# Attention and a two-layer feed-forward on one core: rounded score products for two more pairs, longer score runs, a later decay scaling and another order table

## The chip, the cores and the metric

The kernel runs on one core of one Trainium2 chip. The metric is the device time of one execution in microseconds (us). The engines are TensorE (PE; its weight loads are shown apart, as PEld), VectorE (DVE), ScalarE (ACT), GpSimd (POOL) and SyncE (SP), which here issues most DMA transfers.

## The reference

Eight batches of eight heads, 576 positions, head size 64. The attention has a decay: the logarithm of a gate `f` is summed along the sequence, and the difference of the sums at query and key is added to the score. The output of the attention, 4608 rows of 512, goes through two matrices with a leaky activation between them.

```python
scores = scale * np.matmul(q, k.transpose(0, 1, 3, 2))
log_f = np.log(np.clip(f, 0.0001, 1.0))
cum = np.cumsum(log_f, axis=-1)
decay = cum[:, :, :, None] - cum[:, :, None, :]
scores = np.where(causal, -1e9, scores + decay)
attn = np.exp(scores - scores.max(-1)); attn = attn / (attn.sum(-1) + 1e-9)
x = np.matmul(attn, v)            # then to (4608, 512)
h = x @ w_in
g = np.maximum(h, 0.0) + alpha * np.minimum(h, 0.0)
out = g @ w_out
```

## The kernel before

The work comes in 32 pairs: two heads of one batch, four pairs a batch. Eight batches make eight blocks of 512 rows for the feed-forward (the first 512 positions of each), and the last 64 positions of all batches make a ninth. `attention(n)` issues pair n, `ffn1(b)` the first matrix for block b, `ffn2(u)` the second.

A pair's queries are four tiles of 128 and a tail: tile i has 128(i+1) keys on or under the diagonal, so its scores are 128(i+1) columns for each head. The two heads' scores use 64 rows of the array each; the tail holds the last 64 queries of both heads and uses all 128 rows. Each tile then goes to DVE (line 830, tail line 680), which adds the decay and the mask from `Z` and takes the row extreme in one instruction, and to ACT (line 637) for the exponential and its sum. Pairs 0 to 7 turn the result by PE transposes through PSUM (line 651, `L876` for the tail), with evacuations on ACT and, for the first four pairs, partly on DVE (line 646). Pairs 8 and later turn it by DVE transposes and DMA. The values follow (`big,vr` or `wr,vr` in the rows), the division (`quotients`, line 939), and a split of the result into a rounded part (ACT, line 941) and the rest (POOL, line 943), which are the operands `xx` of the feed-forward.

Scores are computed in one of two ways. A pair under `NN` multiplies `q` and `k` as they are loaded (`rqk`), in float32. Another pair first splits them: ACT copies `q` and `k` into rounded tensors `Qh`, `Kh` (line 590), POOL subtracts to get the rest, `Ql`, `Kl` (line 595), and the scores are the sum of the three products Qh Kh, Qh Kl and Ql Kh; tile 0 of such a pair is done in float32 from a small copy (`qk`, lines 586 and 587). `NN` is 8 here, so pairs 0 to 7 use float32.

A run of scores is one planned operation on PE. `stretch` makes it for pairs under 8: for the first four (`NE`) tiles 0 and 1, then tile 2, then tile 3; for pairs 4 to 7 tiles 0, 1 and 3, then tile 2. Each tile of a run has its own PSUM, and tiles 2 and 3 use a bank per head.

The weights `w_in` come as 64-bit words and are converted block by block (`split64`, lines 364 to 377: four instructions on DVE, two on ACT, two on POOL for each of 16 blocks).

The order of work is made by a planner when the program is built. Every operation has an engine, an estimated duration, dependencies, buffers and a key. The planner takes, over all engines, the operation that can start first, and among those of one engine that could start alike the one with the lowest key. Pair n has key 10n plus offsets; the table `SHIFT` adds a number for each kind of step and pair: L loads, D decay, Z masks, S split, A scores, T transposes, V values, Q quotients, X outputs, W conversion of a weight block (key 40 + 2f for block f). Up to 82 us of its own planned time, where the planner sees a gap over 0.5 us before a PE operation that takes a new bank, it writes matmuls of the identity into it (line 479). The engines then run their queues in that order and wait for each other by semaphores.

The decay starts the program: `f` is loaded, clipped, its logarithm taken on ACT, and DVE sums along the sequence (line 403). DVE multiplies the sums by -8 (line 408), SP stores them to DRAM as `c8` (line 410), and five more DMAs regroup them there as `c8p` for pairs 8 and 9 (line 411). Pairs 1 to 7 read `c8` back, broadcast over the partitions (lines 533, 575). Pair 0 does not: PE spreads its sums from `cu` (line 523), and DVE adds the mask (line 550, `m1`).

Of the kernel before, what the change touches and what calls it, by code (L numbers as in the profile page):

```python
# [222 lines left out]
def attention_moe(  # L223
# [1170 lines left out]
```

## Time and profile before

| | |
|---|---|
| time, median of 3 runs | 991.21 us (990.93 to 991.32) |
| the profiled execution | 990.63 us, its span 988.8 us |
| PE busy | 982.2 us (99%) |
| DVE, ACT, POOL busy | 830.7, 614.4, 375.5 us |
| TensorE's granted clock | 1.000 of full speed over the span |

A busy share says how long an engine had an instruction under way, not whether the result was of use: a matmul of the identity in a gap counts as busy. Ends of matmuls are modelled, so the length of a run of matmuls overlaps the start of the next; from one row's start to the next row's start is how long PE was taken by it. An arrow in brackets gives the idle time before an instruction and what ended it.

### The profile page before, as it was taken

To read this page: it belongs to the slowest core of one execution; us is meant where nothing else is said; L and a number is where in the kernel's file an instruction comes from. 1 tells how busy PE (TensorE), PEld (TensorE's weight loads), DVE (VectorE), ACT (ScalarE), POOL (GpSimd) and SP (SyncE) were. 2 spreads that over 40 slices of the span, in tenths; PEclk is the share of its full clock that TensorE was granted. 3 is DMA by queue.
4 is the path that set the end of the run, shared out by engine and by line. 5 is a ranking of instruction groups with operands and counts; after the bars stand their busy time and mean duration, and the time that the engine had idled before them with its cause. 6 is when DMAs were issued, how large, how long until landed. Compare 5 with 4: busy or idle time off the path is not lost.

```text
span 988.8 us, 20133 instructions
## 1 busy us (share of the span) xinstructions
PE 982.2 (99%) x6935; PEld 827.5 (84%) x6935; DVE 830.7 (84%) x1585; ACT 614.4 (62%) x1399; POOL 375.5 (38%) x652
## 2 busy tenths in 40 slices
PE   9999999999999999999999999999999999999998
PEld 5777788888888888888888888999888988898898
DVE  6899988878787778779637988789999999999995
ACT  7888887878677686767635655645444543544352
POOL 5465976888868797777350000000000000000000
PEclk9999999999999999999999999999999999999999
DMA  7977768888888798796757655553444344334521
GB/s 216 260 215 259 251 217 247 254 246 262 247 251 255 224 261 249 219 267 200 215 180 237 203 172 200 174 170 107 149 128 149 107 149 155 122 107 149 169 67 43
DMA packets 133876, 191.68 MB, mean 194 GB/s; under 512 B 22647, under 2 KB 84590, under 8 KB 133774
## 3 DMA queue, kind: packets, MB, share of 16 engines
q1 hardware_dynamic: 128878, 175.73, 57.2%
q0 software_dynamic: 4608, 14.46, 5.3%
q8 instruction: 55, 0.90, 0.4%
q14 instruction: 47, 0.39, 0.1%
q10 hardware_dynamic: 288, 0.20, 0.1%
HBM read 102.95 MB, written 48.67 MB: 153 GB/s over the span
## 4 chain that ended last, share of the span: by engine, by line
PE 96%; DVE 2%; issue 1%; DMA 0%; ACT 0%; DVEq 0%; ACTq 0%
PE bank L381 93%; PE bank L651 2%; PE bank L444 0%; DMA wr<-in_w_in_dram 0%; DVE xs L939 0%; DVE hs L371 0%; DVE big L830 0%; PE bank L729 0%; PE bank L479 0%; DVE hs L1316 0%; DVE big L646 0%; DVE hs L368 0%; DVE wr L371 0%; DVE hs L367 0%; DVE wr L368 0%
## 5 line engine op out<-in xcount | busy, mean ns | idle before, releaser
L381 PE MATMUL bank<-xx,wi 128*128 128x512 f32 x1728 | 407.2, 392 | 0.0
L381 PEld LDWEIGHTS bank<-xx,wi 128*128 128x128 f32 x1728 | 320.4, 188 | 69.6 <-issue 3.0
L637 ACT ACTIVATE big<-big,st 128x384 f32<-128x384 f32 (+4 forms) x272 | 157.7, 582 | 25.8 <-DVE st L830 24.2
L1029 DVE SCALAR_TENSOR_TENSOR hs<-bank,sa,hs 128x512 f32<-128x512 f32 x116 | 86.5, 745 | 54.0 <-ACT hs L1027 52.5
L1027 ACT ACTIVATE hs<-bank,ab 128x512 f32<-128x512 f32 x116 | 79.7, 687 | 70.6 <-PE bank L381 69.0
L830 DVE CUSTOM_DVE_ANT_0 big<-bank,Z 128x384 f32<-128x384 f32 (+1 forms) x220 | 93.0, 480 | 34.2 <-PE bank L381 27.7
L1268 ACT ACTIVATE xx<-gj 128x1792 fp32r<-128x1792 f32 x37 | 62.4, 1701 | 95.0 <-DVE gj L1261 57.3
L381 PE MATMUL bank<-wot,xx 128*128 128x256 f32 (+1 forms) x734 | 120.6, 323 | 0.0
L381 PE MATMUL bank<-wi,xx 128*128 128x256 f32 (+1 forms) x734 | 120.6, 323 | 0.0
L381 PEld LDWEIGHTS bank<-wi,xx 128*128 128x128 f32 x734 | 106.8, 189 | 12.2
L381 PEld LDWEIGHTS bank<-wot,xx 128*128 128x128 f32 x734 | 106.8, 189 | 12.2
L846 DVE STREAM_TRANSPOSE big<-big 128x768 f32<-128x768 f32 x96 | 90.3, 959 | 8.5 <-ACT big L637 8.5
L543 POOL TENSOR_TENSOR Z<-Z,tri 128x128 f32<-128x128 f32 x192 | 79.8, 444 | 34.3 <-DVE Z L513 30.7
L1269 DVE TENSOR_TENSOR xx<-gj,xx 128x1792 fp32r<-128x1792 f32 x37 | 74.4, 2018 | 2.5 <-ACT xx L1268 2.5
L943 POOL TENSOR_TENSOR xx<-xs,xx 128x256 fp32r<-128x256 f32 x64 | 49.0, 781 | 43.2 <-ACT xx L941 42.7
L381 PEld LDWEIGHTS bank<-big,vr 128*64 128x64 f32 x1168 | 53.7, 137 | 9.1 <-issue 5.5
L381 PE MATMUL bank<-wi,gh 128*128 128x256 f32 (+1 forms) x370 | 60.9, 322 | 0.0
L381 PE MATMUL bank<-wot,gh 128*128 128x256 f32 (+1 forms) x370 | 60.9, 322 | 0.0
L381 PE MATMUL bank<-big,vr 128*64 128x128 f32 (+1 forms) x1168 | 59.7, 260 | 0.0
L381 PEld LDWEIGHTS bank<-wot,gh 128*128 128x128 f32 x370 | 53.9, 189 | 6.0
L381 PEld LDWEIGHTS bank<-wi,gh 128*128 128x128 f32 x370 | 53.9, 189 | 6.0
L1298 ACT ACTIVATE hs<-bank 128x256 f32<-128x256 f32 x102 | 36.5, 384 | 24.9 <-PE bank L381 24.6
(164 smaller groups left out, 1585.6 us busy)
## 6 DMA issues: line engine op xcount, KB each, us to landing
hd<-hs SPq DMA_DIRECT2D x144, 256.0 KB
gj<-hd SPq DMA_DIRECT2D x50, 512.0 KB
rqk<-in_qk_dram SPq DMA_DIRECT2D x28, 512.0 KB
wx<-hd SPq DMA_DIRECT2D x22, 512.0 KB
vr<-in_vv_dram SPq DMA_DIRECT2D x32, 320.0 KB
wr<-in_w_in_dram SPq DMA_DIRECT2D x16, 512.0 KB
wx<-in_w_out_dram SPq DMA_DIRECT2D x16, 512.0 KB
out_dram<-hs SPq DMA_DIRECT2D x30, 256.0 KB
```

The costliest lines, as they stand in the source:

```text
L381: pe.matmul(o, lhsT, rhs, start=start, stop=stop)
L543: ms.append(op("POOL", c_po(128), lambda to=to, i=i, zd=zd: po.tensor_tensor(to()[:, :, -1:], zd()[:, :, i : i + 1], tk(), ALU.add), kc + ...
L637: ex = op("ACT", c_exp(w), lambda: ac.activation(at(bt.t), at(bt.t), AF.Exp, bias=lo()[:, col : col + 1], scale=-1.0, accum_out=su()[:, co ...
L651: pe.transpose(t[:, c : c + 128], src[:, 128 * j : 128 * j + 128], ident)
L830: ve.tensor_tensor_reduce(out=o if turned else blk(o), in0=blk(bS.t[:, c0 : c0 + w]), in1=in1(), scale=-0.125, scalar=3.0e38, op0=ALU.add, ...
L846: ve.transpose(part(b_[:, 0 : 768 if k < 3 else MW]), part(bE.t[:, c0 : c0 + (768 if k < 3 else MW)]))
L943: xl = op("POOL", c_po(256), lambda r=r, t0=t0: po.tensor_tensor(bx.t[:, 1, t0 : t0 + 256], bxs[r].t[:, 0:256], bx.t[:, 0, t0 : t0 + 256]. ...
L1027: cp = op("ACT", c_act(512), lambda bh=bh, bs=bs, fc=fc: ac.activation(bs.t, bh.t, AF.Relu, scale=ab[:, fc : fc + 1]), -1000, [last, o_sg] ...
L1029: cp = op("DVE", c_dve(512), lambda bh=bh, bs=bs, fc=fc: ve.scalar_tensor_tensor(bs.t, bh.t, sa[:, fc : fc + 1], bs.t, ALU.mult, ALU.add), ...
L1268: hi = op("ACT", c_acs(896 * GW), lambda w=w, bgh=bgh: ac.activation(bgh.t[:, 0], w(), AF.Copy), key, [o2], [bj, bgh])
L1269: lo = op("DVE", c_dve(896 * GW), lambda w=w, bgh=bgh: tt(bgh.t[:, 1], w(), bgh.t[:, 0].bitcast(F32), ALU.subtract), key + 0.1, [hi], [bj, ...
L1298: side = op("ACT", c_act(256), lambda m=m, slot=slot: ac.activation(bs.t[:, slot], bo[m].t[:, 256:512], AF.Copy), kd, [last], [bo[m], bs])
```

## The change

- `NN` goes from 8 to 6: pairs 6 and 7 split `q` and `k` and score by three rounded products, tile 0 in float32. Their split on POOL is cut in three pieces, and the small copy for tile 0 takes the first 128 keys, as these pairs' keys stand in plain order.
- Pairs 0 to 3 get the score runs that pairs 4 to 7 have.
- The multiplication by -8, the store of `c8` and the regrouping are issued after pair 0's operations, and the multiplication also waits for pair 0's first masked decay.
- The instruction that brings ACT's table for the exponential reads its own cell, not the decay's buffer.
- The table `SHIFT` has other numbers throughout.

```diff
-NN = 8
+NN = 6
...
-SHIFT = {
+SHIFT = {
...
-('A', 3): 165.1
-('A', 4): 13.0
-('A', 6): 173.3
-('A', 7): 218.4
+('A', 3): -13.3
+('A', 4): 74.5
+('A', 6): 1.9
+('A', 7): 70.1
...
-    o_warm = op("ACT", 1500, lambda: ac.activation(warm, ft()[0:1, 0:1], AF.Exp), -99, o_ln, [bft])
+    o_warm = op("ACT", 1500, lambda: ac.activation(warm, warm, AF.Exp), -99, o_ln)
...
-    o_8 = [op("DVE", 150 + (a1 - a0) / 1.92, lambda a0=a0, a1=a1: ve.tensor_scalar_mul(ft()[:, a0:a1], cu()[:, a0:a1], -8.0),
-              -100, [o_sc[i]], [bcu, bft]) for i, (a0, a1) in enumerate(PC)]
-    o_c8 = op("SP", 400, lambda: sy.dma_start(c8, ft()), -49, o_8, [bft], kb=147)
-    o_c8p = [...
...
+                first_m.append(m1)
...
-                    k0_().rearrange("p (k x) -> p k x", k=4), k_()[:, 0:512].rearrange("p (k x) -> p k x", k=4)[:, :, 0:32]), kc, l_qk, [bqk, bQ])]
+                    k0_().rearrange("p (k x) -> p k x", k=4), (k_()[:, 0:512].rearrange("p (k x) -> p k x", k=4)[:, :, 0:32] if n >= NX[0] else k_()[:, 0:128].rearrange("p (k x) -> p k x", k=4))), kc, l_qk, [bqk, bQ])]
...
-                short = turned and i == 0
+                short = len(terms) > 3 and i == 0
...
-        for tiles in ((0, 1), (2,), (3,)) if n < NE else ((2, 3, 0, 1),) if turned else ((0, 1, 3), (2,)):
+        for tiles in ((0, 1, 3), (2,)) if n < NE else ((2, 3, 0, 1),) if turned else ((0, 1, 3), (2,)):
...
     attention(0)
     op("-", 0, lambda: setattr(plan, "fill", fill), 0, [o_id] + first_up)
+    plan.at("", 0)
+    o_8 = [op("DVE", 150 + (a1 - a0) / 1.92, lambda a0=a0, a1=a1: ve.tensor_scalar_mul(ft()[:, a0:a1], cu()[:, a0:a1], -8.0),
+              -100, [o_sc[i], first_m[0]], [bcu, bft]) for i, (a0, a1) in enumerate(PC)]
+    o_c8 = op("SP", 400, lambda: sy.dma_start(c8, ft()), -49, o_8, [bft], kb=147)
+    o_c8p = [...
```

## Rows read from the trace of the kernel before

**Rows 1.** Page, part 1: busy us (share of the span) x instructions, by engine

```profile
PE 982.2 (99%) x6935; PEld 827.5 (84%) x6935; DVE 830.7 (84%) x1585; ACT 614.4 (62%) x1399; POOL 375.5 (38%) x652
```

**Rows 2.** Busy time by stretches: window, us, then each engine's busy us

```profile
40.00:59.00 19.00, 17.71 (x191) 13.42 (x189) 18.26 (x45) 13.69 (x39) 11.23 (x14) 1.00 0.70 223
59.00:97.00 38.00, 38.00 (x296) 29.63 (x296) 34.65 (x82) 34.28 (x95) 26.05 (x32) 1.00 0.77 243
97.00:124.00 27.00, 26.48 (x176) 20.56 (x176) 24.33 (x42) 22.69 (x59) 26.18 (x32) 1.00 0.81 256
145.00:545.00 400.00, 400.00 (x3224) 332.89 (x3223) 304.39 (x746) 280.20 (x789) 277.40 (x492) 1.00 0.81 238
```

**Rows 3.** Timeline of PE, pair 2's three runs: start us, length us, what

```profile
23.85 0.93 PE L381 MATMUL bank<-rqk 64*128 64x128 f32 x8
...
25.73 0.92 PE L381 MATMUL bank<-rqk 64*128 64x384 f32 x4
...
28.90 1.13 PE L381 MATMUL bank<-rqk 64*128 64x512 f32 x4
```

**Rows 4.** Timeline of PE, pair 6's scores and what follows them

```profile
77.04 1.78 PE L381 MATMUL bank<-rqk 64*128 64x128 f32 x12
78.75 0.28 PE L729 MATMUL bank<-ident,st 128*9 128x128 f32 x1
...
82.65 0.60 PE L381 MATMUL bank<-rqk 128*128 128x256 f32 x2
83.09 0.49 PE L651 MATMUL bank<-ident,big 128*128 128x128 f32 x3
83.42 0.70 PE L381 MATMUL bank<-rqk 128*128 128x320 f32 x2
83.96 0.27 PE L729 MATMUL bank<-ident,st 128*9 128x128 f32 x1
...
88.93 0.92 PE L381 MATMUL bank<-rqk 64*128 64x384 f32 x4
```

**Rows 5.** Timeline of PE, a later pair's rounded scores: first row, and next work

```profile
160.39 0.39 PE L381 MATMUL bank<-Kh,Qh 64*128 64x256 f32 x2
...
163.31 8.35 PE L381 MATMUL bank<-xx,wi 128*128 128x512 f32 x36
```

**Rows 6.** Timeline of PE, 45 to 60 us: stalls, identity matmuls, first feed-forward

```profile
45.53 0.83 PE L479 MATMUL bank<-ident 128*128 128x128 f32 x6
...
48.66 0.66 PE L651 MATMUL bank<-ident,big 128*128 128x128 f32 x4 [0.33 <-ACT big L637]
...
50.68 0.66 PE L651 MATMUL bank<-ident,big 128*128 128x128 f32 x4 [0.93 <-ACT big L637]
...
51.91 1.83 PE L479 MATMUL bank<-ident 128*128 128x128 f32 x14
...
59.01 1.66 PE L381 MATMUL bank<-xx,wi 128*128 128x512 f32 x6
```

**Rows 7.** One tile's instructions (rqk): count, ns minimum/median/maximum, first and last start

```profile
L590 ACT ACTIVATE Qh<-rqk x24: 615/619/628, 97.4 to 465.9; 128x512 fp32r<-128x512 f32 x24
...
L590 ACT ACTIVATE Kh<-rqk x24: 668/672/680, 97.9 to 467.2; 128x576 fp32r<-128x576 f32 x24
L595 POOL TENSOR_TENSOR Ql<-rqk,Qh x24: 1267/1298/1720, 98.1 to 471.3; 128x512 fp32r<-128x512 f32 x24
L595 POOL TENSOR_TENSOR Kl<-rqk,Kh x24: 1404/1435/1869, 99.7 to 472.5; 128x576 fp32r<-128x576 f32 x24
```

**Rows 8.** Timeline of all engines, opening: decay scaling and pair 1's first mask

```profile
6.13 0.62 DVE L408 TENSOR_SCALAR big<-big 64x256 f32<-64x256 f32 x2 [0.20 <-ACT warm L401]
...
6.77 0.43 DVE L550 TENSOR_TENSOR Z<-bank,tri 128x256 f32<-128x256 f32 x1
...
13.22 0.67 POOL L557 TENSOR_TENSOR Z<-Z,tri 128x256 f32<-128x256 f32 x1 [2.33 <-DMA Z<-c]
```

**Rows 9.** One line's instructions: DVE's L368, ns minimum/median/maximum

```profile
L368 DVE SCALAR_TENSOR_TENSOR hs<-wr,hs x8: 692/749/1105, 43.3 to 125.2; 128x512 uint32<-128x512 uint32 x8
```

More of the change, by code (lines that the diff above doesn't have):

```diff
@@ L54 @@
 KD, KE = 100.55, 102
-SHIFT = {('L', 0): 9.4, ('D', 0): 2.2, ('Z', 0): 60.6, ('A', 0): 2.2, ('T', 0): -0.3, ('V', 0): -13.3, ('Q', 0): 36.2, ('X', 0): -10.8, ('L', 1): 26.8, ('D', 1): 1.4, ('Z', 1): -27.5, ('A', 1): 47.1, ('T', 1): 17.0, ('V', 1): 48.8, ('X', 1): 122.0, ('L', 2): 28.7, ('D', 2): 45.5, ('Z', 2): 10.6, ('A', 2): 54.0, ('T', 2): 1.8, ('V', 2): 58.1, ('Q', 2): -44.8, ('X', 2): 24.9, ('L', 3): 15.8, ('D', 3): -69.7, ('Z', 3): 0.9, ('A', 3): 165.1, ('T', 3): -84.7, ('Q', 3): 0.7, ('D', 4): -10.7, ('Z', 4): 63.2, ('A', 4): 13.0, ('T', 4): 4.2, ('V', 3): 35.9, ('Q', 4): 132.1, ('X', 3): -15.3, ('L', 5): 81.7, ('D', 5): -4.2, ('Z', 5): -0.4, ('A', 5): 21.2, ('T', 5): -65.7, ('V', 4): 1.3, ('Q', 5): -3.4, ('X', 4): 18.4, ('L', 6): 69.8, ('D', 6): 30.4, ('A', 6): 173.3, ('T', 6): 64.2, ('V', 5): 16.9, ('L', 7): 15.0, ('D', 7): -6.8, ('Z', 7): -95.9, ('A', 7): 218.4, ('T', 7): 47.3, ('V', 6): -17.7, ('V', 7): -37.7, ('Q', 7): -7.0, ('X', 5): -14.8, ('X', 6): -7.2, ('W', 0): 14.3, ('W', 1): 178.8, ('W', 2): 130.1, ('W', 3): -7.0, ('W', 4): 29.0, ('W', 5): 13.1, ('W', 6): 131.9, ('W', 7): -0.1, ('W', 8): -24.7, ('W', 9): 48.7, ('W', 10): -21.0, ('W', 11): -226.7, ('W', 12): -27.8, ('W', 13): 9.3, ('W', 14): 110.8, ('W', 15): 19.8, ('L', 8): -132.0, ('D', 8): -70.2, ('Z', 8): -11.8, ('S', 8): 10.0, ('A', 8): 59.0, ('L', 9): 6.4, ('D', 9): -6.1, ('Z', 9): 32.3, ('S', 9): -81.3, ('A', 9): -1.9, ('Q', 9): -96.4, ('X', 7): 3.1, ('L', 10): 50.1, ('Z', 10): 7.2, ('S', 10): 75.8, ('A', 10): -14.4, ('V', 8): -29.5, ('L', 11): 6.9, ('Z', 11): 41.4, ('S', 11): -6.8, ('A', 11): -68.7, ('V', 9): 12.9, ('Q', 11): 10.9, ('X', 8): 37.3, ('X', 9): 119.6, ('L', 12): 6.3, ('Z', 12): -18.6, ('S', 12): 23.7, ('A', 12): -9.9, ('V', 10): -2.9, ('L', 13): 2.6, ('Z', 13): -3.7, ('S', 13): 27.4, ('A', 13): 27.1, ('V', 11): -0.8, ('Q', 13): -134.7, ('X', 10): 5.7, ('X', 11): 5.8, ('L', 14): 1.6, ('Z', 14): 459.3, ('S', 14): -32.6, ('A', 14): -10.4, ('V', 12): 1.0, ('L', 15): 34.3, ('Z', 15): 17.4, ('S', 15): 96.4, ('A', 15): -40.5, ('V', 13): -69.9, ('Q', 15): -38.3, ('X', 13): 4.3, ('L', 16): 2.7, ('Z', 16): -198.9, ('S', 16): -187.7, ('A', 16): 154.9, ('V', 14): -18.6, ('L', 17): -9.2, ('Z', 17): 0.6, ('S', 17): 49.4, ('A', 17): -109.5, ('Q', 17): -229.2, ('X', 14): 26.2, ('X', 15): -29.2, ('L', 18): -40.0, ('Z', 18): -30.3, ('S', 18): 19.5, ('A', 18): -44.4, ('V', 16): 8.7, ('L', 19): -4.1, ('Z', 19): 16.8, ('S', 19): -29.0, ('A', 19): -99.9, ('V', 17): -19.8, ('Q', 19): -113.9, ('X', 16): 4.8, ('X', 17): -2.5, ('L', 20): -18.2, ('Z', 20): -4.1, ('S', 20): 3.5, ('A', 20): -15.6, ('V', 18): -13.2, ('L', 21): 24.2, ('Z', 21): -5.1, ('S', 21): 30.9, ('A', 21): 1.5, ('V', 19): -12.3, ('Q', 21): -6.5, ('X', 18): -66.7, ('X', 19): 21.5, ('L', 22): -197.2, ('Z', 22): -25.6, ('S', 22): -118.4, ('A', 22): 52.2, ('V', 20): 46.3, ('L', 23): 3.6, ('Z', 23): 49.0, ('S', 23): 3.0, ('A', 23): -4.3, ('V', 21): 106.1, ('Q', 23): -43.7, ('X', 20): 27.7, ('X', 21): -18.4, ('L', 24): -6.9, ('Z', 24): 91.0, ('S', 24): 17.4, ('A', 24): 103.3, ('V', 22): -23.4, ('L', 25): -7.9, ('Z', 25): 14.7, ('S', 25): -51.9, ('A', 25): 20.7, ('V', 23): 21.8, ('Q', 25): 14.2, ('X', 22): 35.9, ('X', 23): -3.3, ('L', 26): -42.8, ('Z', 26): 29.2, ('S', 26): 11.4, ('A', 26): 78.5, ('V', 24): 156.6, ('L', 27): -38.3, ('Z', 27): 1.9, ('S', 27): 40.9, ('A', 27): 0.5, ('Q', 27): 2.0, ('X', 24): -6.8, ('X', 25): 12.5, ('L', 28): -1.5, ('Z', 28): -21.7, ('S', 28): 28.1, ('A', 28): -23.8, ('V', 26): 13.8, ('L', 29): 6.3, ('Z', 29): -5.4, ('S', 29): -109.1, ('A', 29): -4.1, ('V', 27): -32.8, ('Q', 29): -0.6, ('X', 26): -3.0, ('X', 27): -14.3, ('L', 30): -20.4, ('Z', 30): 3.6, ('S', 30): 13.5, ('A', 30): 40.4, ('V', 28): 9.6, ('L', 31): -7.6, ('Z', 31): -99.0, ('S', 31): 13.9, ('A', 31): -1.5, ('V', 29): 16.7, ('V', 31): 16.3, ('V', 30): -2.0, ('Q', 31): -48.0, ('X', 28): -51.3, ('X', 29): -14.3, ('X', 30): -12.2, ('X', 31): -79.3}
@@ new lines @@
+SHIFT = {('L', 0): 10.0, ('D', 0): 94.6, ('Z', 0): 8.1, ('A', 0): 78.0, ('T', 0): -16.6, ('V', 0): -26.9, ('Q', 0): -47.4, ('X', 0): 116.6, ('L', 1): 21.9, ('D', 1): 109.0, ('Z', 1): -11.9, ('A', 1): 7.3, ('T', 1): -9.1, ('V', 1): -9.5, ('Q', 1): 2.2, ('X', 1): 49.7, ('L', 2): -10.2, ('D', 2): 208.8, ('Z', 2): -23.4, ('A', 2): 5.6, ('T', 2): 268.3, ('V', 2): 33.8, ('Q', 2): -11.8, ('X', 2): -52.6, ('L', 3): 71.1, ('D', 3): 156.3, ('A', 3): -13.3, ('T', 3): 36.7, ('Q', 3): 19.2, ('L', 4): 0.1, ('D', 4): 35.5, ('Z', 4): 47.7, ('A', 4): 74.5, ('T', 4): -56.5, ('V', 3): 0.8, ('Q', 4): -23.7, ('X', 3): 138.0, ('L', 5): 24.5, ('D', 5): -35.8, ('Z', 5): -11.4, ('A', 5): 143.4, ('T', 5): -38.8, ('V', 4): 183.4, ('Q', 5): -48.8, ('X', 4): 55.9, ('L', 6): 162.4, ('D', 6): -18.8, ('Z', 6): 15.2, ('S', 6): -52.8, ('A', 6): 1.9, ('T', 6): -266.1, ('V', 5): -7.1, ('L', 7): -28.9, ('D', 7): 86.5, ('Z', 7): -11.4, ('S', 7): -16.2, ('A', 7): 70.1, ('T', 7): 121.7, ('V', 6): 496.0, ('V', 7): -3.1, ('Q', 7): -41.8, ('X', 5): 198.8, ('X', 6): 54.2, ('W', 0): -63.0, ('W', 1): 384.4, ('W', 2): 117.4, ('W', 3): -12.1, ('W', 4): 171.4, ('W', 5): 120.2, ('W', 6): -145.9, ('W', 7): -49.0, ('W', 8): 31.1, ('W', 9): -37.8, ('W', 10): -0.6, ('W', 11): 110.4, ('W', 12): 4.9, ('W', 13): -13.9, ('W', 14): -11.3, ('W', 15): 47.0, ('L', 8): 416.4, ('D', 8): -19.3, ('Z', 8): 4.1, ('S', 8): -34.1, ('A', 8): 198.7, ('L', 9): -41.2, ('D', 9): -46.3, ('Z', 9): -5.5, ('S', 9): 192.4, ('A', 9): -9.5, ('Q', 9): -33.8, ('X', 7): 39.0, ('L', 10): 6.5, ('Z', 10): 37.1, ('S', 10): 76.4, ('A', 10): -57.8, ('V', 8): 3.5, ('L', 11): 62.0, ('Z', 11): -43.5, ('S', 11): 77.1, ('A', 11): -0.2, ('Q', 11): -47.7, ('X', 8): 5.7, ('X', 9): -25.3, ('L', 12): -33.0, ('Z', 12): 13.1, ('A', 12): 31.0, ('V', 10): 29.9, ('L', 13): -4.4, ('Z', 13): -13.6, ('S', 13): -5.3, ('A', 13): -4.4, ('V', 11): 1.0, ('Q', 13): -10.5, ('X', 10): 17.6, ('L', 14): 50.0, ('Z', 14): 87.5, ('S', 14): 6.4, ('A', 14): -16.8, ('V', 12): -28.4, ('L', 15): -175.7, ('Z', 15): 105.2, ('S', 15): 12.3, ('A', 15): 4.9, ('V', 13): -44.6, ('Q', 15): 5.6, ('X', 12): -95.8, ('X', 13): 98.2, ('L', 16): 22.6, ('Z', 16): 0.8, ('S', 16): 24.1, ('A', 16): -141.7, ('V', 14): 29.7, ('L', 17): 24.8, ('Z', 17): -5.1, ('S', 17): -139.9, ('A', 17): 15.8, ('V', 15): 0.5, ('Q', 17): 18.8, ('X', 14): -20.0, ('X', 15): -29.9, ('L', 18): 41.8, ('Z', 18): -12.8, ('S', 18): 10.7, ('A', 18): -4.1, ('V', 16): 6.5, ('L', 19): -81.0, ('Z', 19): -6.3, ('S', 19): 17.9, ('A', 19): 21.7, ('V', 17): 0.1, ('Q', 19): -94.5, ('X', 16): 32.4, ('X', 17): 22.1, ('L', 20): -5.3, ('Z', 20): -10.0, ('S', 20): 3.0, ('A', 20): -10.3, ('V', 18): 25.8, ('L', 21): -43.3, ('Z', 21): 51.2, ('S', 21): 4.0, ('A', 21): 8.9, ('V', 19): -0.8, ('Q', 21): -14.1, ('X', 18): 17.7, ('X', 19): -12.0, ('L', 22): -37.2, ('S', 22): 2.5, ('A', 22): 6.3, ('V', 20): 15.6, ('L', 23): 88.2, ('Z', 23): -20.9, ('S', 23): 164.0, ('A', 23): 75.0, ('V', 21): -20.9, ('Q', 23): 13.1, ('X', 20): 86.4, ('X', 21): -23.2, ('L', 24): 0.8, ('Z', 24): 9.6, ('S', 24): 253.1, ('A', 24): -6.8, ('V', 22): 0.8, ('L', 25): 93.5, ('Z', 25): -3.8, ('S', 25): -1.2, ('A', 25): 22.1, ('V', 23): 21.4, ('Q', 25): -98.9, ('X', 22): -3.5, ('X', 23): 23.4, ('L', 26): -23.3, ('Z', 26): 21.9, ('S', 26): -1.4, ('A', 26): -1.0, ('V', 24): 58.8, ('L', 27): -7.2, ('Z', 27): -27.4, ('S', 27): 39.4, ('A', 27): -134.6, ('V', 25): -44.8, ('Q', 27): 0.7, ('X', 24): -12.7, ('X', 25): -35.8, ('L', 28): -0.2, ('Z', 28): -4.3, ('S', 28): 44.6, ('A', 28): 16.1, ('V', 26): -62.7, ('L', 29): 61.4, ('Z', 29): -2.9, ('S', 29): -2.9, ('A', 29): -27.8, ('V', 27): 4.8, ('Q', 29): -24.6, ('X', 26): -2.4, ('X', 27): 24.0, ('L', 30): 4.7, ('Z', 30): 29.4, ('S', 30): 9.7, ('A', 30): -1.9, ('V', 28): -191.9, ('L', 31): -14.6, ('Z', 31): -35.7, ('S', 31): 24.9, ('A', 31): -22.1, ('V', 29): -25.0, ('V', 31): 0.8, ('V', 30): 39.1, ('Q', 31): -16.4, ('X', 28): -6.5, ('X', 29): 6.8, ('X', 30): 24.7, ('X', 31): -32.2}
@@ L406, in attention_moe @@
     o_scan = o_sc[1]
-    o_8 = [op("DVE", 150 + (a1 - a0) / 1.92, lambda a0=a0, a1=a1: ve.tensor_scalar_mul(ft()[:, a0:a1], cu()[:, a0:a1], -8.0),
-              -100, [o_sc[i]], [bcu, bft]) for i, (a0, a1) in enumerate(PC)]
-    o_c8 = op("SP", 400, lambda: sy.dma_start(c8, ft()), -49, o_8, [bft], kb=147)
-    o_c8p = [op("SP", 400, lambda k=k: sy.dma_start(c8p[:, 128 * k : 128 * k + 128].rearrange("p (s c) -> p s c", c=32),
-                                                    c8[:, 0:512].rearrange("p (s k c) -> p s k c", k=4, c=32)[:, :, k]), 6, [o_c8], kb=60) for k in range(4)]
-    o_c8p.append(op("SP", 400, lambda: sy.dma_start(c8p[:, 512:S], c8[:, 512:S]), 6, [o_c8], kb=16))
     o_id = op("POOL", 600, lambda: make_identity(nc, ident), -98)
@@ L479, in fill @@
             pe.matmul(bank[:, 0:128], ident, ident, start=True, stop=True)
-    first_up = []
+    first_up, first_m = [], []
     x_ops, x_late, xt_ops, s_0 = {}, [], [], []
@@ L1036, in attention_moe @@
     op("-", 0, lambda: setattr(plan, "fill", fill), 0, [o_id] + first_up)
+    plan.at("", 0)
+    o_8 = [op("DVE", 150 + (a1 - a0) / 1.92, lambda a0=a0, a1=a1: ve.tensor_scalar_mul(ft()[:, a0:a1], cu()[:, a0:a1], -8.0),
+              -100, [o_sc[i], first_m[0]], [bcu, bft]) for i, (a0, a1) in enumerate(PC)]
+    o_c8 = op("SP", 400, lambda: sy.dma_start(c8, ft()), -49, o_8, [bft], kb=147)
+    o_c8p = [op("SP", 400, lambda k=k: sy.dma_start(c8p[:, 128 * k : 128 * k + 128].rearrange("p (s c) -> p s c", c=32),
+                                                    c8[:, 0:512].rearrange("p (s k c) -> p s k c", k=4, c=32)[:, :, k]), 6, [o_c8], kb=60) for k in range(4)]
+    o_c8p.append(op("SP", 400, lambda: sy.dma_start(c8p[:, 512:S], c8[:, 512:S]), 6, [o_c8], kb=16))
     o_sg = None
```

## The prediction

> **What bounds the kernel now.** I read the page's busy line first, then the busy time by stretches of the span, then TensorE's order of instructions in the opening. TensorE (PE) is busy for 982.2 of 988.8 us [rows 1]. By stretches it is full between 59 and 97 us and from 145 to 545 us, and it misses 1.29 us at 40 to 59 and 0.52 us at 97 to 124 [rows 2]. The reader is to see two regimes. From 59 us on, PE always finds something, because the feed-forward of batch 0 lies ready as a stock of work: there a microsecond taken off PE's own instructions is a microsecond off the end. Before 59 us the busy share deceives. The planner writes matmuls of the identity into gaps (line 479); they count as busy and compute nothing. Before pair 3's last transposes and behind them PE shows 0.83 and 1.83 us of such matmuls and 0.33 and 0.93 us of idleness that ends with an exponential on ACT [rows 6]: 3.9 us in which PE waits for pairs 3 and 4. In that stretch DVE is busy for 18.26 of 19.00 us [rows 2], so the waiting is for DVE and for what ACT makes of DVE's output.
>
> **The change part by part.** All terms are made against the profiled execution's own time, 990.63 us (its span of 988.8 and 1.83 around it), which is 0.58 under the median of 991.21; I add that 0.58 at the end.
>
> *Pairs 6 and 7 by rounded products.* Removed: the float32 scores. For pair 6 these are the run of tiles 0, 1 and 3 from 77.04 to 78.75 (1.71 us), the tail's two parts, 82.65 to 83.09 and 83.42 to 83.96 (0.44 and 0.54), and tile 2, 0.92 long, less the 0.07 by which the first run's length overlaps what follows (1.78 against 1.71), 0.85 [rows 4]: 3.54 us. Added: three rounded products per tile, tile 0 staying float32. A later pair that already does this, tails included, runs from 160.39 to 163.31 [rows 5]: 2.92 us. So 0.62 us a pair, 1.2 us in all, on PE, in the stretch in which it is full. Bounds: the whole lengths of the float32 rows (1.78, 0.60, 0.70, 0.92) sum to 4.00, which would give 1.08 a pair and 2.2 us; if the products of pairs 6 and 7 are broken up between other work and lose their overlap, nothing is left. I take -1.2, the start-to-start reading, since PE's next instruction begins there.
>
> *Their cover.* The split of q and k is new for these two pairs: on ACT two copies of 0.62 and 0.67 us, on POOL two subtractions of 1.30 and 1.44 us, here in three pieces each [rows 7], and a small copy on each engine. That is at least 2 x 1.29 = 2.6 us of ACT and 2 x 2.74 = 5.5 us of POOL; at the longest durations of those rows POOL takes 2 x 3.59 = 7.2 us. I cost them at nothing: PE has the feed-forward of batch 0 to do meanwhile, and the results are needed by PE only. If that cover is gone, up to 5.5 us (7.2 at most) comes back. It is thin on one side: POOL is busy for 26.18 of 27.00 us at 97 to 124, but for 26.05 of 38.00 at 59 to 97 [rows 2], so it matters whether the table puts the split early. It does: the keys of the scores are 10 per pair plus the table's entry, for pair 6 233 before and 62 after, for pair 7 288 and 140.
>
> *The first four pairs in two runs.* Pair 2's three runs last 0.93, 0.92 and 1.13 us [rows 3], 2.98 together; pair 6's two for the same tiles 1.78 and 0.92 [rows 4], 2.70. So 0.28 us a pair, 1.1 us for four. But PE waits in this stretch anyway, so a part only makes its wait longer; between 0 and -1.1 I take -0.5. Against it: a run of tiles 0, 1 and 3 asks for four banks of PSUM at one time, where each run asked for two.
>
> *The new table.* It decides the order of everything before 545 us. What I can tie to a row: pair 3 is the last that batch 0's feed-forward needs, and its scores had key 30 + 165 = 195, behind pair 4's 40 + 13 = 53; now they have 17 against 115. The stall of 3.9 us [rows 6] is the wait for pairs 3 and 4, and DVE there alternates between them and the weights' conversion. Bounds: all of the 3.9 recovered, or as much again lost where another pair comes late in its place. I take -1.0, a quarter of it, because DVE's own work, 18.26 of 19.00 us [rows 2], is not removed and only its order changes.
>
> *The decay scaling later.* The two multiplications by -8 (0.62 us on DVE [rows 8]) move behind pair 0's first masked decay, so the store of the scaled decay and pair 1's broadcasts of it, all on SP's queue, leave later, and so do the five regrouping copies behind them. POOL waited 2.33 us for the first of those broadcasts [rows 8], so pair 1's masks come later by nearly what the store does: 0.43 us for the masked decay that now goes ahead [rows 8], plus at most one 0.62. Pair 0 gains at most the 0.62. Bounds -0.6 to +1.1 us; I take +0.2, nearer to zero, because PE is still busy with pair 0 when pair 1's masks land. The activation-table warm-up reads its own cell instead of the decay; it stays behind the logarithms on ACT, and I cost it at nothing: it hides behind the scan on DVE, and without that cover it is inside the 0.6 already counted.
>
> Sum: 990.63 - 1.2 - 0.5 - 1.0 + 0.2 = 988.1 us, and with 0.58 for the median 988.7 us, a gain of 2.5 us or 0.25%. About 0.2%, 2.0 us, is what a measurement of this kernel can tell from no change, so faster means under 989.2 and slower over 993.2.
>
> **The rivals.** *Nothing is won before 59 us:* the order changes, the wait moves to another pair, and only the rounded products remain: 991.2 - 1.2 = 990.0 us. For it speaks that DVE is nearly full at 40 to 59; against it, that 2.66 us of PE's time there is identity matmuls.
>
> *DVE is held by the added POOL work.* One form of the weights' conversion on DVE takes between 692 and 1105 ns for the same 128x512 [rows 9], while POOL works beside it: 0.41 us longer at worst. The split adds 14 POOL instructions; if each lengthens one DVE instruction so, DVE loses 5.7 us, and its idle time at 59 to 124 is 3.35 + 2.67 = 6.0 us [rows 2]. So it is just covered if spread evenly; if half passes through, 2.9 us come back: 991.6 us. The Trainium skill, "SBUF — State Buffer", section "Who interferes with whom", says that a VectorE instruction with two SBUF inputs contends with a GpSimd instruction that reads SBUF, and that the later one is blocked for the other's whole instruction. By that rule, which the spread of that row fits, the change adds collisions and this rival gains weight; what speaks against it is that ACT and POOL feed PE here with a stock of work in between.
>
> *The inputs of batch 1 come late (slower).* Batch 1's feed-forward needs the outputs of pairs 4 to 7. If the split's 5.5 us of POOL work lands in the full stretch at 97 to 124 [rows 2], the scores of pair 7, its values and the division behind them shift by that, and PE, at the end of batch 0's feed-forward, has no stock left but later pairs' scores, which need the same POOL. The whole price is 5.5 us: 988.7 + 5.5 = 994.2. It decides once more than 4.5 us of it passes through, that is, once pair 7's output comes later than PE's last matmul of batch 0 by so much. For it: POOL's 97% share. Against it: both pairs' earlier keys.
>
> *The stall before 59 us nearly goes:* 2.9 more of the 3.9 us: 985.8 us. For it: pair 3's key; against it: DVE's share.
>
> **How the numbers follow.** The forecast has 0.48, its own range 987.0 to 990.2, of which 0.39 lie under 989.2 and 0.09 above. Nothing won early: 0.15. DVE held: 0.08. Late inputs: 0.20. Stall gone: 0.09. Faster is 0.39 + 0.09 = 0.48, same 0.09 + 0.15 + 0.08 = 0.32, slower 0.20. The range reaches from 985.0 (the stall gone, with half of the float32 rows' overlap) to 994.0 (late inputs, most of the price); it leaves out about half of the slow case and a little of the fast one, 0.14.
>
> **What would show it.** In the changed profile pair 6's and 7's scores should be rounded products that sum to about 2.9 us a pair; the first four pairs should each show the 64-row matmuls of tiles 0, 1 and 3 in one piece of about 1.8 us; line 479 should show less than the 0.83 and 1.83 us before the feed-forward, whose first matmul stands at 59.01 [rows 6] and should come one to two microseconds earlier. PE should stay full from there to 545 us; idleness at 135 to 150 us before a feed-forward matmul would be the late inputs. The prediction is wrong if the identity matmuls and idle time before the feed-forward grow, or if PE shows new gaps between 60 and 150 us.

## The result: 996.8 us, slower by 5.7 us

The changed kernel took 996.78 us (median; 996.43 to 998.4) beside 991.07 us for the kernel before on the same chip: a ratio of 1.0059, 95% interval [1.0047, 1.0071]. The forecast was 988.7 with a range to 994.0; both its direction and its range failed. The profiled execution took 996.43 us, its span 994.6.

First the page's busy line (columns as in [rows 1]) and its group for the feed-forward's multiplication; the last column is the idle time of PE just before it and what ended most of that.

```profile
PE 981.8 (99%) x6943; PEld 828.0 (83%) x6943; DVE 831.6 (84%) x1585; ACT 615.8 (62%) x1405; POOL 383.6 (39%) x666
L381 PE MATMUL bank<-xx,wi 128*128 128x512 f32 x1728 | 407.3, 392 | 5.2 <-POOL wi L377 2.6
```

PE has as much to do as before (982.2 us [rows 1]); the span grew by idle time. The same group before:

```profile
L381 PE MATMUL bank<-xx,wi 128*128 128x512 f32 x1728 | 407.2, 392 | 0.0
```

Lines of the new kernel lie some five lower than in the rows of before (L377 stayed, L830 is L825, L943 is L938). The windows, with the columns of [rows 2], tell where:

```profile
40.00:59.00 19.00, 17.68 (x194) 13.57 (x192) 17.65 (x48) 16.31 (x51) 10.53 (x15) 1.00 0.77 233
59.00:97.00 38.00, 37.35 (x302) 29.87 (x302) 31.29 (x71) 35.09 (x97) 31.99 (x43) 1.00 0.83 256
97.00:124.00 27.00, 27.00 (x236) 22.05 (x235) 24.43 (x53) 25.16 (x69) 22.26 (x31) 1.00 0.85 259
124.00:145.00 21.00, 17.85 (x105) 12.91 (x100) 18.10 (x35) 13.84 (x36) 18.62 (x22) 1.00 0.73 235
145.00:545.00 400.00, 397.94 (x3213) 330.75 (x3212) 307.92 (x749) 279.47 (x790) 279.21 (x504) 1.00 0.81 235
```

The kernel before, at 124 to 145 us:

```profile
124.00:145.00 21.00, 21.00 (x165) 16.71 (x164) 17.47 (x43) 17.35 (x50) 14.86 (x31) 1.00 0.62 207
```

Before 59 us nothing was won. From 124 us on, where PE was full before, it now misses 3.15 and 2.06 us; at 59 to 97 it misses 0.65. POOL's busy time at 59 to 97 rose from 26.05 [rows 2] to 31.99, and at 97 to 124 it fell from 26.18 to 22.26. PE's timeline names the waits (start, length, what, idle before it):

```profile
59.15 1.20 PE L381 MATMUL bank<-xx,wi 128*128 128x512 f32 x4
...
137.67 3.96 PE L381 MATMUL bank<-xx,wi 128*128 128x512 f32 x16 [2.58 <-POOL wi L377]
...
144.68 4.74 PE L381 MATMUL bank<-xx,wi 128*128 128x512 f32 x18 [0.57 <-ACT wi L376]
151.39 4.38 PE L381 MATMUL bank<-xx,wi 128*128 128x512 f32 x18 [1.97 <-ACT hs L1019]
```

The first feed-forward starts at 59.15, not earlier than 59.01 [rows 6]. Three waits, 5.1 us together, follow between 135 and 152 us. Two are for `w_in`: PE ran out of converted weight blocks, whose subtraction is on POOL. The third is for an ACT instruction that empties a bank. ACT's own timeline shows what that one was queued behind; DVE's and POOL's show what went on when it was held up:

```profile
150.00 0.76 ACT L936 ACTIVATE xx<-xs 128x256 fp32r<-128x256 f32 x2 [2.69 <-DVE xs L934]
150.67 0.67 ACT L1019 ACTIVATE hs<-bank,sg 128x512 f32<-128x512 f32 x1
```
```profile
147.03 3.28 DVE L934 TENSOR_TENSOR xs<-xs,ri 128x256 f32<-128x256 f32 x2
```
```profile
146.62 2.74 POOL L537 TENSOR_TENSOR Z<-Z,tri 128x128 f32<-128x128 f32 x7
```

Two instructions of DVE with two inputs took 3.28 us, more than twice the 1.39 us that the same two take elsewhere (e4, at 103.24 us). The first alone took 2.88 us, while POOL added masks; ACT waited for it, and the eviction stood behind on ACT's queue. That the masks held it is read from the times; no run takes them away.

### The profile page after: what moved, and what is told of

Same layout as the page of the kernel before. It is cut to its first block, busy times and chain, and to the rows that moved or that the text cites. A ratio compares the mean times of both kernels' runs of the same rounds, so it can differ in the third digit from the quotient of the medians.

```text
span 994.6 us, 20168 instructions
## 1 busy us (share of the span) xinstructions
PE 981.8 (99%) x6943; PEld 828.0 (83%) x6943; DVE 831.6 (84%) x1585; ACT 615.8 (62%) x1405; POOL 383.6 (39%) x666
## 4 chain that ended last, share of the span: by engine, by line
PE 87%; DVE 6%; DMA 3%; issue 1%; ACT 1%; POOL 1%; SPq 1%; DVEq 0%; POOLq 0%; ACTq 0%
PE bank L381 86%; DVE xs L934 1%; DVE big L825 1%; DMA Zt<-c8p 1%; DMA rqk<-in_qk_dram 1%; DMA Zt<-c 1%; PE bank L646 0%; DVE hs L367 0%; PE bank L438 0%; DVE hs L368 0%; DMA vr<-in_vv_dram 0%; DVE big L675 0%; DMA Z<-c 0%; POOL Z L537 0%; ACT big L632 0%
## 5 line engine op out<-in xcount | busy, mean ns | idle before, releaser
L632 ACT ACTIVATE big<-big,st 128x128 f32<-128x128 f32 (+4 forms) x272 | 157.7, 581 | 29.9 <-DVE st L825 27.8
L825 DVE CUSTOM_DVE_ANT_0 big<-bank,Z 128x384 f32<-128x384 f32 (+1 forms) x220 | 92.7, 479 | 41.5 <-PE bank L381 34.6
L938 POOL TENSOR_TENSOR xx<-xs,xx 128x256 fp32r<-128x256 f32 x64 | 49.6, 789 | 56.6 <-ACT xx L936 55.1
```

The costliest lines, as they stand in the source:

```text
L632: ex = op("ACT", c_exp(w), lambda: ac.activation(at(bt.t), at(bt.t), AF.Exp, bias=lo()[:, col : col + 1], scale=-1.0, accum_out=su()[:, co ...
L825: ve.tensor_tensor_reduce(out=o if turned else blk(o), in0=blk(bS.t[:, c0 : c0 + w]), in1=in1(), scale=-0.125, scalar=3.0e38, op0=ALU.add, ...
L938: xl = op("POOL", c_po(256), lambda r=r, t0=t0: po.tensor_tensor(bx.t[:, 1, t0 : t0 + 256], bxs[r].t[:, 0:256], bx.t[:, 0, t0 : t0 + 256]. ...
```

## The experiments

Theories at the start: T1, the weights' loads come late; T2, the split of pairs 6 and 7 delays the conversion on POOL and DVE; T3, the order that the planner makes, not the added work. Ratios are to the kernel before, measured beside each run; its own median lay between 990.4 and 991.07 us, so medians of different experiments compare to some tenths only.

**e1 and e2, the loads.** `load_w_in` waits for `s_0[6]`, the seventh score run: with three runs a pair it is pair 2's first, with two pair 3's. The loads start at 40.5 us after, 27.7 before. e1 ties them to an earlier run, e2 gives the changed kernel its three runs back.

```diff
-    ... CONV0 + CONV * fc, [s_0[6]], [])
+    ... CONV0 + CONV * fc, [s_0[4]], [])          # e1
-        for tiles in ((0, 1, 3), (2,)) if n < NE else ...
+        for tiles in ((0, 1), (2,), (3,)) if n < NE else ...   # e2
```

> The changed kernel, but the weights' loads wait for the fifth run of scores instead of the seventh, so again for pair 2's first run, as in the kernel before. Theory 1 (the loads hang on a run counted by its place in a list, the two-run form moved that place to pair 3, the weights come some 12 us later and PE runs dry at 135 to 151 us): first weight load at about 28 us instead of 40.5, the 5.2 us of waiting at 135 to 151 gone, 989 to 992 us. Theory 2 (the split of pairs 6 and 7 fills POOL and holds DVE, so the weights' conversion ends late): the wait stays, 995 to 998. Theory 3 (the new table's order alone): 995 to 998.

> The changed kernel with the first four pairs' scores in three runs again; the seventh run is then pair 2's first by itself. Theory 1: first weight load at about 28 us, no wait at 135 to 151, 990 to 993 us (up to 1 us above the kernel with only the dependency put back, for the third run's switches). Theories 2 and 3: 995 to 999.

e1: 1011.26 us, 1.0206 [1.0189, 1.0223], loads from 29.4 us. e2: 1013.55, 1.0228 [1.0213, 1.0243], loads from 28.4 us. Both moved the loads forward and came out 14.5 and 16.8 us over the changed kernel, outside all that was expected. About half of that is waits, the longest of 2.5 to 6.4 us for `xx` from POOL; the other half is PE's own busy time, 989.0 and 990.6 us against 981.8. Since either edit makes the planner write every queue anew, they don't price the loads alone; they show only that early loads were no cure in these two orders.

**e3, late loads in the kernel before** (`s_0[6]` to `s_0[9]`).

> The kernel before with one edit: the weights' loads wait for the tenth run of scores, pair 3's first, where they waited for the seventh, pair 2's first. Theory 1: the loads start about 10 us later, PE waits for weights between 125 and 155 us, 994 to 998 us. Theories 2 and 3: nothing of theirs is in this kernel, 990 to 992.

995.34 us, 1.0049 [1.0032, 1.0066]; loads from 30.9 us, and no wait for weights. PE's longest wait beside the one of 1.5 us at the start, which all versions have, is 2.7 us for an ACT instruction (line 925). The cost has another place, so T1 isn't shown by it.

**e4, the change without the rounded products.**

```diff
-NN = 6
+NN = 8
```

> The changed kernel with pairs 6 and 7 scored in float32 again, so without their split. Theory 1: the loads stay late and the wait stays; PE has about 1 us more of its own: 996 to 999 us. Theory 2: POOL and DVE are free for the conversion, 990 to 993. Theory 3: 996 to 999.

991.61 us, 1.0002 [0.9990, 1.0015]. The two runs, the late loads (from 39.4 us), the later decay scaling and the new table together cost and gain nothing that can be told from the spread. The whole loss comes with `NN = 6`. T1 falls as far as late loads alone should cost; whether earlier loads would have taken up the split, in an order otherwise the same, wasn't tried.

**e5 and e6, work taken out of the changed kernel, its order kept.** e5 leaves out POOL's twelve subtractions for pairs 6 and 7, so the rests of q and k, whose three products then all use the rounded parts. e6 leaves out one of DVE's four instructions for each weight block, so the low bits of `w_in`.

```diff
-                out.append(op("POOL", ..., lambda ...: po.tensor_tensor(
+                out.append(op("POOL", ..., lambda ...: n < NX[0] or po.tensor_tensor(     # e5
...
-            ve.scalar_tensor_tensor(a(), lo(), 29, a(), ALU.logical_shift_right, ALU.bitwise_or)   # e6
```

> The changed kernel with the order of every queue kept, but POOL's twelve subtractions for pairs 6 and 7 are not issued, and their three products all use the rounded parts, so PE's work is the same and these scores are only the rounded ones. Theory 2 (the split's time on POOL, and what it holds up on DVE, makes the weights' conversion late, and PE runs dry at 135 to 151 us): the last conversion on POOL ends at about 140 us instead of 146, the wait of 5.2 us shrinks to under 1.5, 991 to 993 us. Theory 3 (the order into which the planner puts things once the split is there, not its time): the wait stays, 995 to 997 us.

> The changed kernel with the order of every queue kept, but one of the four DVE instructions of the weights' conversion (line 371) is not issued in any of the 16 blocks, so the low bits of the weights are missing and DVE has some 13 us less to do before 146 us. If the weights' conversion is what PE runs dry on (theories 1 and 2): the wait at 135 to 151 goes, 990 to 993 us. If PE waits there for something else, such as the outputs of pairs 4 to 7: 995 to 997 us.

e5: 995.38 us, 1.0052 [1.0037, 1.0067], with 2.4 and 1.7 us of the waits still there: by medians 1.4 us less than the changed kernel, by ratios 0.7, where T3 had put it. e6: 993.27 us, 1.0020 [1.0007, 1.0033]; the wait for POOL's `wi` falls from 2.58 to 0.26 us, the one for ACT's is gone, the 2.0 us behind the division stay. So the weights' conversion did set PE's pace at 135 to 145 us, and it was late mostly for another reason than POOL's subtractions.

**e7 and e8, one part alone in the kernel before:** `NN = 6` with what it needs, or the two runs.

> The kernel before with one part of the change alone: pairs 6 and 7 score by rounded products; runs, table and decay scaling as before. Theory 2: the split's 9 us on POOL delay the weights' conversion here too, PE waits for them between 120 and 155 us, 993 to 997 us. Theory 3 (only the new table's order has no room for it): 989.5 to 991.5 us, PE's own work being 0.5 to 1.2 us less.

> The kernel before with one part of the change alone: the first four pairs' scores in two runs, so that the seventh run, on which the weights' loads hang, is pair 3's. Theory 1 in its strong form (late loads alone cost): 994 to 998 us, with waits for weights. Otherwise, as in the run with the loads moved by hand, waits elsewhere or none: 990 to 995 us.

e7: 1007.69 us, 1.0173 [1.0158, 1.0188]. e8: 1011.37, 1.0205 [1.0188, 1.0222]. Both are far over what any theory gave. Under the old table each part alone costs more than the whole change under the new one.

**e9, rounded products in the order of e4.** The planner is told that pairs 6 and 7 are float32; the split's instructions stand where they fit, at no planned time. Every engine's queue is that of e4, but for the inserted instructions and the products.

```diff
+        free = n < NX[0]
...
-            o1 = op("ACT", c_acs(w - z), ...
+            o1 = op("-" if free else "ACT", 0 if free else c_acs(w - z), ...
```

> The changed kernel's rounded products for pairs 6 and 7, but every other instruction stands in the order that it has in the kernel with all first eight pairs in float32 (991.6 us); the split's instructions are put into that order at no planned time. Theory 3 (the wait comes from the order that the planner makes around the split, not from the split's work): 990 to 992 us; TensorE 0.4 to 1.2 us less busy, no wait of over 1 us for the weights' conversion. Theory 2 (the split's time on GpSimd and on VectorE beside it delays the conversion): 995 to 997 us, with waits of 2 us or more for the conversion on GpSimd between 124 and 150 us.

994.42 us, 1.0030 [1.0020, 1.0040]: between both theories. Against the changed kernel the order gives back 2.4 us by medians; against e4 2.8 us stay, with no other order to blame. Since the queues are alike, the two timelines can be laid side by side (e9's lines lie up to three higher). POOL of e4, then of e9:

```profile
66.91 0.74 POOL L377 TENSOR_TENSOR wi<-wr,wi 128x256 fp32r<-128x256 f32 x1 [1.68 <-ACT wi L376]
...
68.94 1.44 POOL L377 TENSOR_TENSOR wi<-hs,wi 128x256 fp32r<-128x256 f32 x2 [0.21 <-ACT wi L376]
```
```profile
66.21 2.33 POOL L591 TENSOR_TENSOR Ql<-rqk,Qh 128x170 fp32r<-128x170 f32 x3 [0.82 <-ACT Qh L586]
68.49 0.28 POOL L583 COPY qk<-rqk 128x128 f32<-128x128 f32 x1
68.74 1.71 POOL L591 TENSOR_TENSOR Kl<-rqk,Kh 128x192 fp32r<-128x192 f32 x3
70.41 0.73 POOL L377 TENSOR_TENSOR wi<-wr,wi 128x256 fp32r<-128x256 f32 x1
...
71.73 1.42 POOL L377 TENSOR_TENSOR wi<-hs,wi 128x256 fp32r<-128x256 f32 x2
```

The weight blocks' subtractions stand 2.8 to 3.5 us later, behind the split of pair 6. DVE of e4, then of e9, at the next block and the next tile:

```profile
71.50 0.42 DVE L367 TENSOR_SCALAR hs<-wr 128x512 uint32<-128x512 uint32 x1
...
78.09 0.54 DVE L825 CUSTOM_DVE_ANT_0 big<-bank,Z 128x384 f32<-128x384 f32 x1
```
```profile
73.19 0.88 DVE L367 TENSOR_SCALAR hs<-wr 128x512 uint32<-128x512 uint32 x1 [2.18 <-POOL wi L377]
...
79.27 1.10 DVE L371 SCALAR_TENSOR_TENSOR wr<-wr 128x512 uint32<-128x512 uint32 x1
...
81.42 0.54 DVE L828 CUSTOM_DVE_ANT_0 big<-bank,Z 128x384 f32<-128x384 f32 x1
```

DVE waits for the buffer that POOL frees late, a conversion takes 1.10 us beside POOL where the same step took 0.69 in e4 (at 76.33 us), and the tile behind them comes 3.3 us later. PE of e4, then of e9, from a feed-forward row ahead of pair 6's scores to pair 7's values:

```profile
76.97 1.63 PE L381 MATMUL bank<-xx,wi 128*128 128x512 f32 x6
...
104.17 2.98 PE L381 MATMUL bank<-big,vr 128*64 128x128 f32 x56
```
```profile
77.02 1.86 PE L381 MATMUL bank<-xx,wi 128*128 128x512 f32 x6
...
82.03 0.39 PE L381 MATMUL bank<-Kh,Qh 128*128 128x256 f32 x1 [1.25 <-DVE st L828]
...
102.96 0.41 PE L381 MATMUL bank<-Kh,Qh 128*128 128x320 f32 x1 [0.16 <-ACT hs L1022]
...
105.70 2.98 PE L381 MATMUL bank<-big,vr 128*64 128x128 f32 x56
```

From row to row e4 needs 27.20 us without a wait, e9 28.68, of which 1.41 are waits: 27.27. On PE the rounded products save nothing. The 1.25 us are a wait for the bank that the late tile on DVE frees. PE's list of waits in e9 has none for `wi`: with the order held, the split's cost reaches PE through DVE's queue, not through missing weights.

**e10 and e12, fewer identity matmuls** (`FILL` from 82 to 35, in e9's kernel and in the one before).

> As e9, with the identity matmuls allowed to 35 us of planned time only and no longer to 82, so that the group at about 52 us goes. If those matmuls push useful work back, the first feed-forward matmul comes up to 0.9 us earlier and the time is 0.5 to 0.9 us under e9. If they only fill a wait, the time is that of e9 within 0.2 us; if they keep TensorE's clock up, it is longer and the granted clock after 52 us falls under 1.0.

> The kernel before with the identity matmuls allowed to 35 us of planned time only. If the 1.83 us of them at 51.91 us hold up the multiplication behind them, 0.3 to 0.9 us less than before, with the first feed-forward matmul at 58.1 to 58.7 us. If they fill a wait, 991 us within 0.2; if they keep the clock up, longer, with a granted clock under 1.0 after 52 us.

e10: 994.30 us, 1.0030 [1.0019, 1.0041], as e9. e12: 991.59, 1.0006 [0.9994, 1.0017], no gain; its rows are in the section on the hardware.

**e11, the whole change with the table of before.**

> The changed kernel's whole structure with the table of the kernel before. Theory 3 (a table fits one structure; any other order made from it leaves late inputs): 1005 to 1015 us, waits of 3 us or more between 140 and 170 us, as in the kernels with a part of the change and that table. If the table were a small matter, as the prediction had it (1 us): 997 to 999 us.

1008.4 us, 1.0170 [1.0146, 1.0193]: for this structure the new table is worth 11.6 us by medians.

**e13 and e14, e9 taken apart.** What stayed open was which part of the split costs the 2.8 us. e13 leaves POOL's subtractions out of e9 (the same rests as in e5), e14 keeps the whole split but scores in float32.

```diff
-                out.append(op("-" if free else "POOL", ..., lambda ...: po.tensor_tensor(
+                out.append(op("-" if free else "POOL", ..., lambda ...: n < NX[0] or po.tensor_tensor(   # e13
...
+            return l_qk, rz, rt, bZ, [(lambda a, b: q_()[:, a:b], k_)]                    # e14, if free
```

> e9 (994.4 us) without GpSimd's twelve subtractions for pairs 6 and 7, order otherwise the same; left out of the computation are the rests of q and k of these pairs, so their three products all use the rounded parts. If GpSimd's 9 us of subtractions and what they do to VectorE's conversion are the whole of the 2.8 us by which e9 is longer than the kernel in float32 with the same order: 991.2 to 992.0 us, VectorE about 4 us less busy than in e9, and no wait of 1.2 us at 81 us for a bank that VectorE frees. If ScalarE's four copies or the products themselves are the cause: 993.5 us or more.

> e9 with the split of pairs 6 and 7 issued in full, but their scores in float32 from q and k as loaded, so that nothing reads the split. If the split's work on GpSimd, ScalarE and beside VectorE is the cause and the rounded products give TensorE 0.3 us: 994.4 to 995.0 us. If waiting for the split, or the rounded products themselves, is the cause: 992.5 us or less.

e14: 994.12 us, 1.0035 [1.0021, 1.0049]: the split alone, which nothing reads, costs what e9 costs. So its work is the cause, not the products and not waiting for it. e13: 992.77 us, 1.0025 [1.0017, 1.0034]; the 1.25 us wait is gone and L367 stands at 71.57 again. By medians the subtractions are 1.65 of the 2.8 us, by ratios 0.5, and the intervals overlap: the times don't settle their size.

The traces settle more of it. Up to the first feed-forward matmul the order is the same in e4, e9, e13 and e14, and nothing of the split stands there (its first copy on ACT starts at 65.31 us in e9). Still that matmul starts at 58.23 in e4, 58.20 in e9, 59.02 in e13 and 59.30 in e14 (e4's row, cut at 59 us, then e13's):

```profile
58.23 0.96 PE L381 MATMUL bank<-xx,wi 128*128 128x512 f32 x3
```
```profile
59.02 1.66 PE L381 MATMUL bank<-xx,wi 128*128 128x512 f32 x6
```

So the opening differs by 1.1 us between executions of one order. From this matmul to the end of the span (990.0, 991.4, 991.1 and 992.4 us) the four take 931.8, 933.2, 932.1 and 933.1 us: behind the opening the split costs 1.3 to 1.4 us, of which its subtractions are 1.1 (e9 less e13) and the rest 0.3. In e4 alone PE waits 0.54 us for a DMA at 220.57, so the last figure could be up to 0.5 larger. The other half of the medians' 2.8 us stands in no trace: e9's profiled execution was 1.2 us under its median. ScalarE's copies are left in e13, but weren't tried alone.

The sum by medians: 991.07 to e4 0.5 (not told from nothing), to e13 1.2, to e9 1.65, to the changed kernel 2.4. No version beat the kernel before.

## Why the prediction was wrong

- **The cover (the failed step).** "I cost them at nothing: PE has the feed-forward of batch 0 to do meanwhile, and the results are needed by PE only." The results are; the engines that make them are not idle. On POOL's queue the split stands in front of the weights' subtractions, DVE waits for what these free, the score tiles behind on DVE come 3.3 us later, and PE waits for their bank. e9 and e14 against e4 show the split's work costing 2.5 to 2.8 us by medians with the order held, of which the traces show about half. In the changed kernel's own order the stock itself ran dry too: the feed-forward needs the converted blocks of `w_in`, and PE waited 2.58 and 0.57 us for them; e5 shows that POOL's subtractions were the smaller part of that. The cover's price, 5.5 us on POOL, was itself low: the two splits' rows in e9 (66.21 to 70.4 and 80.40 to 84.3 us) are 8.3 us long (2.33 and 2.02 us for q and 1.71 for k in three pieces, where [rows 7] has 1.30 and 1.44 in one), and POOL's busy time rose by 11.2 us, from 372.7 in e4 to 383.9 in e9.
- **The order (the term of the new table, -1.0).** The prediction summed edits as if the rest stood still. A different split gives the planner different keys and durations, hence other queues: 2.4 us lost here (the changed kernel against e9). Five kernels with a table beside another structure than in the two given kernels are 1.7 to 2.3% over the kernel before (e1, e2, e7, e8, e11). That is no rule: e4 pairs the new table with `NN = 8` and loses nothing, and e3 costs 0.5%. Which exchange in the queues costs the 2.4 us stays open; e6 shows only that DVE's work on the weights is part of it.
- **Rounded products, -1.2.** They gave 0.3 us at most (PE's busy time is 982.4 us in e4, 982.1 in e9). Ends were read start to start [rows 4, 5], and a start depends on what follows: a float32 tail part took 0.44 and 0.54 us ahead of transposes [rows 4], but 0.25 and 0.30 ahead of a feed-forward matmul in e4 (97.78 to 98.03, 101.31 to 101.61), where pair 7's float32 scores sum to 3.11 us. Pair 6's products after, by the same reading, are 3.34 us and pair 7's 3.06, not 2.92. Between the fixed rows in e4 and e9 the saving is nil.
- **The early terms, -0.5, -1.0 and +0.2.** The run of tiles 0, 1 and 3 is 1.78 us, as said. But e4, which has all three, comes out even. Its first feed-forward stands at 58.23 us, 0.78 before the 59.01 of [rows 6]; since the opening differs by 1.1 us between executions, that is not shown to be a gain. The identity matmuls did shrink, from 28 and 3.9 us to 20 and 2.8 us in both e4 and the changed kernel; in the latter PE waits 0.91 us for DVE at 49.93 instead. I also missed that the two runs move `s_0[6]` and with it the loads by 13 us; by e4 that costs nothing alone.
- **The rivals.** The slower one, chance 0.20, came nearest (994.2 against 996.8), by luck, for it had the wrong place: batch 1's inputs. What came late was batch 0's weights and, at 151 us, one eviction. Its sign, idle time at 135 to 150 us, is what appeared. "DVE is held" was right in its term: with the order held DVE's busy time rose from 825.5 (e4) to 830.9 us (e9), 5.4 against the 5.7 given there. The rule named beside it (the Trainium skill, "SBUF — State Buffer", "Who interferes with whom") agrees with that rise, and with its fall to 827.2 us in e13, which leaves out POOL's subtractions; which instruction held which, no run shows.

## What to carry to other kernels

When added work is to hide behind a stock, look at the queues that it joins: what stands behind it there, who waits for that, and who makes the stock's own operands? In a kernel whose queues come from a planner, an edit is a new order first and a new cost second; hold the order and insert the edit, to know which of the two you measure. Price a replaced group between two fixed rows around it, not from its own starts.

## What the runs showed of the hardware

The identity matmuls that I counted as lost time kept the clock up in the kernel before. Its values of a pair take 2.98 us there:

```profile
54.62 2.98 PE L381 MATMUL bank<-big,vr 128*64 128x128 f32 x56
```
Without the group at 51.91 us [rows 6], e12 shows in PE's timeline:

```profile
52.01 0.28 PE L729 MATMUL bank<-ident,st 128*9 128x128 f32 x1 [0.75 <-DVE st L727]
52.22 2.15 PE L381 MATMUL bank<-rqk 64*128 64x384 f32 x4
54.30 3.83 PE L381 MATMUL bank<-big,vr 128*64 128x128 f32 x56
...
59.53 1.66 PE L381 MATMUL bank<-xx,wi 128*128 128x512 f32 x6
```
and in its windows (the column after POOL is the granted clock):

```profile
52.00:54.00 2.00, 1.99 (x5) 0.88 (x5) 1.82 (x11) 1.85 (x9) 0.00 (x0) 0.67 0.78 263
54.00:56.00 2.00, 2.00 (x17) 1.70 (x18) 1.97 (x6) 2.00 (x6) 1.56 (x3) 0.50 0.72 173
56.00:59.00 3.00, 3.00 (x52) 2.68 (x49) 2.86 (x6) 1.03 (x4) 0.99 (x1) 0.99 0.69 217
```

Behind waits of 0.93 (at 50.07) and 0.75 us the clock falls to 0.50, its lower level of 1.2 GHz, and the values of a pair take 3.83 us instead of 2.98. So the fill's 1.83 us bought back about as much: the first feed-forward stands at 59.53, no earlier than 59.01, and the time can't be told from that of the kernel before. It is not so in every order: in e10, where the wait at 50.58 is 0.20 us, the clock stays at 1.00 from 50 to 59 us without such a group, and the values take 2.98 us. Falls of the clock go with the bad orders too: in e8 it averaged 0.66 from 145 to 165 us, and PE's busy time over the span was 989.0 us against 982.2.
